# Heads exchanged in every second pair, and two output banks, in a retention layer ahead of two feed-forward layers

## The chip, the cores and the metric

One Trainium2 chip, one of its cores. The metric is device time in microseconds (us). A row of the profile comes from one profiled execution; the times of the table are those of separate timed runs.

## The reference, cut to what matters

Three layers follow each other on 2 x 768 = 1536 tokens of width 512 (8 heads of 64). Only the first one is touched by the change:

```python
def _attn_ref(q, k, v):            # each (2, 8, 768, 64)
    gamma = 1.0 - 2.0 ** (-5.0 - np.arange(H))
    for t in range(S):
        state = gamma * state + np.einsum('bhd,bhe->bhde', k[:, :, t], v[:, :, t])
        y[:, :, t] = scale * np.einsum('bhd,bhde->bhe', q[:, :, t], state)
# then x = y as (1536, 512);  h = x @ w_in (512 x 2048);  x = (h * tanh(softplus(h))) @ w_out
# then out = (sigmoid(x @ w_gate) * (x @ w_val)) @ w_out2    (512 x 1536 each way)
```

## The kernel before, in words

**The retention layer** is worked in chunks of 128 tokens, 12 of them (six to a batch element), numbered j = 0 to 11. Two heads make a pair, and a pair's two heads (e = 0 and 1) lie on partitions 0 to 63 and 64 to 127 of the tile `qk_t`; four pairs p = 0 to 3 lie side by side. For a chunk the kernel does this, all in plain fp32, and the trace counts two matmul instructions for each such product:

- `at_scores(j)`: the products of k and q, written to two PSUM banks `sc[e]`, 8 products (tile `sc`); on GpSimd, v times its decay (`vp`) and, from the second chunk of a batch element on, the output's decay (`og`); on VectorE the causal mask, which takes both banks to the tile `a`.
- `at_state(j)`: k times v is added to a running state in one bank (tile `st`), 8 products; ScalarE copies the state to SBUF as `s` for chunk j + 1. It is left out for the last chunk of a batch element (j = 5 and 11).
- `at_out(j)`: 8 products of `a` and `vp` go to one output bank `ao`, and, for all but the first chunk of a batch element (10 of the 12), 8 products of the state `s` and q are added to it, each of which uses 64 rows and 64 columns of the 128 x 128 array. VectorE then multiplies the bank with `og` into the activation tile `acc`, 128 x 512 in one instruction.

The output banks come from the pool `ps_o`, which has two buffers, one bank each. The same pool later holds the results of the feed-forward layers' second products (`o1_first`, `o1`, `o2`).

`blocks` runs four chunks at a time. For a chunk j it issues, in this order, `at_scores(j + 1)`, from j = 3 on one step of weight preparation (`pump`), `at_state(j)`, `at_out(j)`, the loads of chunk j + 4 and of a weight piece, and, from j = 4 on, one group of 12 matmuls of the first feed-forward layer (`dense`: tiles `h<-xc` and `h<-B`). The retention tiles of q, k and v have four buffers, so the loads for chunk j + 4 can start when chunk j has been used.

**A step of weight preparation** takes 512 x 128 weights that arrive as 64-bit floats (`raw`), decodes them (one instruction on ScalarE, three on VectorE, of which two are `SCALAR_TENSOR_TENSOR`), and splits the result into two fp32r halves (one copy `w` on ScalarE, one subtraction on VectorE).

**Order.** Through the whole retention stage each engine executes its instructions in program order (the class `InOrder`; in the profile these have the helper's line L66). Behind it (`early.clear`) a planner orders each engine's instructions at build time, and these rows have lines of their own (L109 is the matmul helper of the feed-forward layers). The first work behind the retention stage that uses `ps_o` is `out1_first(0)`, whose four steps `o1_first` take one bank each.

Of the kernel before, what the change touches and what calls it, by code (L numbers as in the profile page):

```python
# [9 lines left out]
F32 = mybir.dt.float32  # L10
# [4 lines left out]
ALU = mybir.AluOpType  # L15
PSUM = bass.MemoryType.PSUM

P = 128
# [4 lines left out]
def kernel(ctx, tc, qk, nv, w1i, w1o, w2g, w2v, w2o, ma_in, og_in, sg_in, ck_in, out):  # L23
# [14 lines left out]
    NP = KK  # L38
    D = P // 2
# [4 lines left out]
    SPC = N // P  # L44
# [27 lines left out]
    pe, dve, act, pool, sync = [InOrder(e) for e in (nc.tensor, nc.vector, nc.scalar, nc.gpsimd, nc.sync)]  # L72
# [8 lines left out]
    ps_o = ctx.enter_context(tc.tile_pool(name="ps_o", bufs=2, space=PSUM))  # L81
# [5 lines left out]
    acc_t = [big.tile([P, KK, N], F32, name=f"acc{c}") for c in range(NCH)]  # L87
# [354 lines left out]
    with ExitStack() as actx:  # L442
# [8 lines left out]
        qk_t, nv_t, a_t, vp_t, og_t, st_t, s_t = {}, {}, {}, {}, {}, {}, {}  # L451
# [32 lines left out]

        def at_out(j):
            a, v, t, s = a_t.pop(j), vp_t[j], qk_t[j], s_t.get(j)
            o = ps_o.tile([P, NP, P], F32, tag="o", name="ao")
            inter = j % SPB > 0

            for p in range(NP):  # L490
                for e in range(2):
                    pe.matmul(
                        out=o[D * e:D * e + D, p, :], lhsT=v[:, 2 * p + e, :], rhs=a[:, e, p, :],
                        start=p == 0, stop=p == NP - 1 and not inter, skip_group_check=True,
                    )
            if inter:
                for p in range(NP):
                    for e in range(2):
                        r = slice(D * e, D * e + D)
                        pe.matmul(  # L500
                            out=o[r, p, :], lhsT=s[r, p, :], rhs=t[r, 0, p, :], start=False, stop=p == NP - 1,
                            skip_group_check=True,
                        )
            dve.tensor_tensor(
                out=acc_t[j // SPC][:, :, j % SPC * P:j % SPC * P + P], in0=o, in1=og_t[j], op=ALU.mult
            )

        def at_state(j):
            if j % SPB == SPB - 1:
                return  # L510
            v, k = vp_t[j], nv_t[j]
            if j % SPB == 0:
                st_t[0] = ps_s.tile([P, NP, D], F32, tag="s", name="st")
            st = st_t[0]
            for p in range(NP):
                for e in range(2):
                    pe.matmul(
                        out=st[D * e:D * e + D, p, :], lhsT=k[:, 0, 2 * p + e, :], rhs=v[:, 2 * p + e, :],
                        start=j % SPB == 0 and p == 0, stop=p == NP - 1, skip_group_check=True,
                    )  # L520
            s_t[j + 1] = at.tile([P, NP, D], F32, tag="s", name="s")
            act.activation(out=s_t[j + 1], in_=st, func=AF.Copy)

        def fin(j):
            at_state(j)
            at_out(j)
# [22 lines left out]
        for n in range(WARM):  # L549
            o = ps_o.tile([P, NP * D], F32, tag="o", name="warm")  # L550
# [109 lines left out]
```

## Time and profile before

| | |
|---|---|
| timed runs | median 601.92 us, 600.83 to 603.3 (3 runs) |
| the profiled execution | 603.4 us, its span 601.6 us, so 1.8 us lie around the span |
| mean granted TensorE clock in the span | 0.993 |
| busy share of the span | TensorE matmuls 97%, VectorE 69%, GpSimd 55%, ScalarE 41% |

In the rows, PE is the matmuls of TensorE, PEld its weight loads, DVE is VectorE, ACT ScalarE, POOL GpSimd, SPq the queue that issues DMAs. A matmul row's duration is that of one instruction in a pipeline: rows overlap each other, so the pace is read from starts and not from durations. A tile's name stands as `out<-in`; a bracket behind a row gives the idle time of its engine just before it and what ended it. `issue` in a bracket means that the profile shows no wait that ended there.

### The profile page before, as it was taken

The numbers are of one execution on the slowest core, as the hardware profiler recorded it, in microseconds if no ns is written. First come the engines' busy times: TensorE is split into PE (matmuls) and PEld (weight loads), VectorE is DVE, ScalarE is ACT, GpSimd is POOL, SyncE is SP. The second block draws the span as 40 slices with busy tenths as digits, with TensorE's granted clock in tenths as the row PEclk, the third lists the DMA queues.
The fourth block names the chain that finished last, engine by engine and source line by source line (L and its number), as shares of the span: only waits on it lengthen the run. The fifth ranks groups of instructions, "written<-read, shape, count | busy, mean of one in ns | idle before, by whom it ended". The sixth has DMA issues, their size and how long they took to land.

```text
span 601.6 us, 7973 instructions
## 1 busy us (share of the span) xinstructions
PE 585.4 (97%) x3056; PEld 478.6 (80%) x3056; DVE 416.0 (69%) x572; ACT 249.5 (41%) x433; POOL 331.5 (55%) x268
## 2 busy tenths in 40 slices
PE   8998999999999999998999999999999999999997
PEld 7776787788787888886788787888888888888885
DVE  3899896438959485665776977686578487472554
ACT  1354456545454354443434645642333443333210
POOL 3345556628785585484632556955566657557100
PEclk9999899999999999998999999999999999999999
DMA  9983232204222122401220031133023033000014
GB/s 346 407 286 123 89 106 69 72 0 141 70 71 94 47 70 71 139 4 67 71 70 1 1 106 42 64 105 106 0 81 104 28 95 94 21 1 1 1 53 159
DMA packets 15591, 52.27 MB, mean 87 GB/s; under 512 B 1984, under 2 KB 2112, under 8 KB 15552
## 3 DMA queue, kind: packets, MB, share of 16 engines
q1 hardware_dynamic: 15552, 51.75, 25.0%
q8 instruction: 24, 0.39, 0.3%
q14 instruction: 15, 0.12, 0.1%
HBM read 48.60 MB, written 3.15 MB: 86 GB/s over the span
## 4 chain that ended last, share of the span: by engine, by line
PE 64%; DVE 15%; issue 7%; POOL 6%; DMA 4%; ACT 3%; SPq 0%; POOLq 0%; ACTq 0%; DVEq 0%
PE o L109 29%; PE h L109 27%; PE hx L109 7%; DVE v L102 3%; DMA nv_t<-nv 3%; DVE v L103 2%; DVE v L101 2%; DVE acc L357 2%; POOL w L163 1%; POOL vp L66 1%; POOL g L91 1%; DVE v L66 1%; POOL og L66 1%; POOL g L66 1%; DVE T L91 1%
## 5 line engine op out<-in xcount | busy, mean ns | idle before, releaser
L91 POOL TENSOR_TENSOR g<-e,g 128x512 fp32r<-128x512 f32 x73 | 116.5, 1605 | 86.7 <-ACT g L90 86.7
L109 PE MATMUL o<-g,w 128*128 128x512 f32 x576 | 141.8, 394 | 2.8 <-DVE acc L357 2.6
L109 PEld LDWEIGHTS o<-g,w 128*128 128x128 f32 x576 | 108.7, 190 | 28.2 <-DVE acc L357 5.1
L109 PE MATMUL h<-T,w 128*128 128x512 f32 x444 | 112.6, 390 | 1.1 <-DVE T L91 0.6
L163 POOL TENSOR_TENSOR w<-v,w 128x512 fp32r<-128x512 f32 x56 | 76.2, 1368 | 67.8 <-ACT w L162 67.6
L109 PE MATMUL o<-w,g 128*128 128x512 f32 x432 | 106.0, 390 | 0.0
L109 PEld LDWEIGHTS h<-T,w 128*128 128x128 f32 x444 | 83.2, 188 | 19.4 <-DVE T L91 1.0
L109 PEld LDWEIGHTS o<-w,g 128*128 128x128 f32 x432 | 81.0, 188 | 17.2 <-POOL g L91 0.4
L109 PE MATMUL h<-B,w 128*128 128x512 f32 x348 | 90.8, 390 | 0.8 <-DVE e L347 0.8
L109 PEld LDWEIGHTS h<-B,w 128*128 128x128 f32 x348 | 65.1, 188 | 15.1 <-DVE e L347 1.2
L357 DVE TENSOR_TENSOR acc<-o,acc 128x512 f32<-128x512 f32 x72 | 49.0, 686 | 39.1 <-PE o L109 38.8
L90 ACT ACTIVATE g<-e 128x512 fp32r<-128x512 f32 x77 | 48.1, 631 | 53.5 <-DVE e L347 35.5
L163 POOL TENSOR_TENSOR w<-s,w 128x512 fp32r<-128x512 f32 x34 | 48.1, 1422 | 34.5 <-ACT w L162 34.2
L101 DVE TENSOR_SCALAR v<-v 128x512 int32<-128x512 int32 x59 | 44.7, 761 | 28.2 <-ACT v L100 27.9
L162 ACT ACTIVATE w<-v 128x512 fp32r<-128x512 f32 x59 | 36.8, 631 | 63.0 <-DVE v L103 35.2
L377 DVE TENSOR_TENSOR acc<-o,acc 128x512 f32<-128x512 f32 x60 | 41.1, 686 | 30.8 <-PE o L109 30.4
L100 ACT ACTIVATE v<-raw 128x512 f32<-128x512 f32 x59 | 39.2, 669 | 52.5 <-POOL w L163 20.0
L102 DVE SCALAR_TENSOR_TENSOR v<-raw,v 128x512 int32<-128x512 int32 x59 | 56.0, 950 | 1.0
L103 DVE SCALAR_TENSOR_TENSOR v<-raw,v 128x512 int32<-128x512 int32 x59 | 56.2, 953 | 0.5
L109 PE MATMUL hx<-xc,w 128*128 128x512 f32 x216 | 55.7, 390 | 0.3 <-ACT e L341 0.3
L109 PE MATMUL h<-xc,w 128*128 128x512 f32 x216 | 55.0, 389 | 0.0
L109 PEld LDWEIGHTS hx<-xc,w 128*128 128x128 f32 x216 | 40.5, 188 | 9.2 <-ACT e L341 0.8
(78 smaller groups left out, 611.0 us busy)
## 6 DMA issues: line engine op xcount, KB each, us to landing
raw<-w1i SPq DMA_DIRECT2D x16, 512.0 KB, 3.6
raw<-w1o SPq DMA_DIRECT2D x16, 512.0 KB, 3.4
qk_t<-qk SPq DMA_DIRECT2D x12, 512.0 KB, 6.3
nv_t<-nv SPq DMA_DIRECT2D x12, 512.0 KB, 7.0
raw<-w2g SPq DMA_DIRECT2D x12, 512.0 KB, 3.3
raw<-w2v SPq DMA_DIRECT2D x12, 512.0 KB, 3.4
raw<-w2o SPq DMA_DIRECT2D x12, 512.0 KB, 3.3
out<-acc SPq DMA_DIRECT2D x12, 256.0 KB, 2.0
```

The lines of the kernel that those rows point to most:

```text
L66: i = call(**kw)
L90: act.activation(out=hi, in_=raw, func=AF.Copy)
L91: eng.tensor_tensor(out=lo, in0=raw, in1=hi.bitcast(F32), op=ALU.subtract)
L100: act.activation(out=v, in_=high.bitcast(F32), func=AF.Copy, scale=2.0 ** -112)
L101: dve.tensor_scalar(out=b, in0=b, scalar1=3, scalar2=None, op0=ALU.logical_shift_left)
L102: dve.scalar_tensor_tensor(out=b, in0=low, scalar=29, in1=b, op0=ALU.logical_shift_right, op1=ALU.bitwise_or)
L103: dve.scalar_tensor_tensor(out=b, in0=high, scalar=SIGN, in1=b, op0=ALU.bitwise_and, op1=ALU.bitwise_or)
L109: pe.matmul(out=o, lhsT=w(a), rhs=x(b), start=first and n == 0, stop=last and n == 2, skip_group_check=more)
L162: act.activation(out=hi, in_=v, func=AF.Copy)
L163: late.append(lambda: lo_eng["w"].tensor_tensor(out=lo, in0=v, in1=hi.bitcast(F32), op=ALU.subtract))
L357: dve.tensor_tensor(out=acc, in0=o, in1=acc, op=ALU.add)
L377: dve.tensor_tensor(out=acc, in0=o, in1=acc, op=ALU.add)
```

## The change

In pairs 1 and 3 the two heads change places among the partitions of `qk_t` (done on the host, when the input is laid out). So in those pairs the score bank `sc[e]` holds the other head, the running state is written to the other half of the array's columns, and a product of state and q reads rows of one half and writes columns of the other. In pairs 0 and 2 rows and columns are of the same half, as before. The eight products of state and q of a chunk thus use all four 64 x 64 quarters of the array. The output goes to two banks, pairs 0 and 2 to one, pairs 1 and 3 to the other, 256 columns each, so that no bank is written into the same partitions from both halves of the rows. Both come from `ps_o`. The multiplication with `og` becomes two instructions of 128 x 256, one for a bank.

```diff
         def at_out(j):
             a, v, t, s = a_t.pop(j), vp_t[j], qk_t[j], s_t.get(j)
-            o = ps_o.tile([P, NP, P], F32, tag="o", name="ao")
+            o = [ps_o.tile([P, NP // 2, P], F32, tag="o", name="ao") for _ in range(2)]
             inter = j % SPB > 0
             for p in range(NP):
                 for e in range(2):
                     pe.matmul(
-                        out=o[D * e:D * e + D, p, :], lhsT=v[:, 2 * p + e, :], rhs=a[:, e, p, :],
-                        start=p == 0, stop=p == NP - 1 and not inter, skip_group_check=True,
+                        out=o[p % 2][D * e:D * e + D, p // 2, :], lhsT=v[:, 2 * p + e, :], rhs=a[:, e ^ p % 2, p, :],
+                        start=p < 2, stop=p >= NP - 2 and not inter, skip_group_check=True,
                     )
             if inter:
                 for p in range(NP):
                     for e in range(2):
-                        r = slice(D * e, D * e + D)
+                        r = slice(D * (e ^ p % 2), D * (e ^ p % 2) + D)
                         pe.matmul(
-                            out=o[r, p, :], lhsT=s[r, p, :], rhs=t[r, 0, p, :], start=False, stop=p == NP - 1,
-                            skip_group_check=True,
+                            out=o[p % 2][D * e:D * e + D, p // 2, :], lhsT=s[r, p, :], rhs=t[r, 0, p, :],
+                            start=False, stop=p >= NP - 2, skip_group_check=True,
                         )
-            dve.tensor_tensor(
-                out=acc_t[j // SPC][:, :, j % SPC * P:j % SPC * P + P], in0=o, in1=og_t[j], op=ALU.mult
-            )
+            for n in range(2):
+                dve.tensor_tensor(
+                    out=acc_t[j // SPC][:, n::2, j % SPC * P:j % SPC * P + P], in0=o[n], in1=og_t[j][:, n::2],
+                    op=ALU.mult,
+                )
         def at_state(j):
...
             for p in range(NP):
                 for e in range(2):
+                    r = e ^ p % 2
                     pe.matmul(
-                        out=st[D * e:D * e + D, p, :], lhsT=k[:, 0, 2 * p + e, :], rhs=v[:, 2 * p + e, :],
+                        out=st[D * r:D * r + D, p, :], lhsT=k[:, 0, 2 * p + e, :], rhs=v[:, 2 * p + e, :],
                         start=j % SPB == 0 and p == 0, stop=p == NP - 1, skip_group_check=True,
                     )
...
     def feature_major(a):
-        a = a.reshape(B, H // 2, 2, nsub, P, D).transpose(0, 3, 2, 5, 1, 4)
+        a = a.reshape(B, H // 2, 2, nsub, P, D)
+        a = np.stack([a[:, p, ::1 - p % 2 * 2] for p in range(H // 2)], axis=1).transpose(0, 3, 2, 5, 1, 4)
         return a.reshape(B * nsub, 2 * D, H // 2, P)
```

## Rows read from the trace of the kernel before

**Rows 1.** The page's first part: busy us, share of the span, instructions.

```profile
PE 585.4 (97%) x3056; PEld 478.6 (80%) x3056; DVE 416.0 (69%) x572; ACT 249.5 (41%) x433; POOL 331.5 (55%) x268
```

**Rows 2.** Busy us (instructions) by stretch: PE, PEld, DVE, ACT, POOL; clock; DMA.

```profile
10.50:25.70 15.20, 14.54 (x260) 12.58 (x256) 10.44 (x16) 4.98 (x10) 8.99 (x9) 1.00 1.02 407
25.70:59.10 33.40, 29.26 (x302) 23.09 (x301) 31.58 (x42) 13.21 (x27) 14.52 (x11) 1.00 0.65 231
59.10:77.58 18.48, 18.47 (x181) 14.86 (x181) 15.46 (x20) 8.15 (x15) 9.10 (x7) 0.91 0.25 86
77.58:601.60 524.02, 514.39 (x2245) 421.01 (x2243) 355.65 (x491) 221.26 (x380) 296.38 (x235) 0.99 0.19 64
```

**Rows 3.** Timeline, chunk j = 2 on PE: start, us, what, count.

```profile
14.17 1.16 PE L66 MATMUL sc<-qk_t 64*128 64x128 f32 x16
...
15.26 0.69 PE L66 MATMUL st<-vp,nv_t 128*64 128x64 f32 x16
...
15.77 1.05 PE L66 MATMUL ao<-a,vp 128*64 128x128 f32 x16
...
16.75 1.09 PE L66 MATMUL ao<-qk_t,s 64*64 64x128 f32 x16
...
17.77 1.16 PE L66 MATMUL sc<-qk_t 64*128 64x128 f32 x16
```

**Rows 4.** Timeline of PE cut to 16.76 to 16.90 us.

```profile
16.75 0.33 PE L66 MATMUL ao<-qk_t,s 64*64 64x128 f32 x2
```

**Rows 5.** Timeline of ACT, 18 to 24 us.

```profile
19.52 0.70 ACT L66 ACTIVATE v<-raw 128x512 f32<-128x512 f32 x1 [3.08 <-DMA raw<-w1i]
...
22.73 0.36 ACT L66 ACTIVATE s<-st 128x256 f32<-128x256 f32 x1
```

**Rows 6.** Timeline of PE, 20 to 30 us: the state product of j = 4.

```profile
23.19 0.69 PE L66 MATMUL st<-vp,nv_t 128*64 128x64 f32 x16 [0.66 <-issue]
```

**Rows 7.** Timeline of DVE, 37.4 to 49.1 us: one chunk's work.

```profile
43.76 1.28 DVE L66 TENSOR_TENSOR a<-sc,ma 128x512 f32<-128x512 f32 x2
45.15 1.02 DVE L66 TENSOR_SCALAR v<-v 128x512 int32<-128x512 int32 x1
46.20 2.86 DVE L66 SCALAR_TENSOR_TENSOR v<-raw,v 128x512 int32<-128x512 int32 x2
48.98 0.68 DVE L66 TENSOR_TENSOR acc<-ao,og 128x512 f32<-128x512 f32 x1
```

**Rows 8.** Timeline of ACT, 56 to 60 us.

```profile
58.11 0.63 ACT L66 ACTIVATE w<-v 128x512 fp32r<-128x512 f32 x1 [4.33 <-DVE v L66]
58.65 0.37 ACT L66 ACTIVATE s<-st 128x256 f32<-128x256 f32 x1
```

**Rows 9.** Timeline of PE, 59 to 78 us: j = 9, 11, and out1_first.

```profile
59.11 0.69 PE L66 MATMUL st<-vp,nv_t 128*64 128x64 f32 x16 [2.40 <-issue]
...
60.76 1.97 PE L66 MATMUL ao<-qk_t,s 64*64 64x128 f32 x16
...
72.68 1.09 PE L66 MATMUL ao<-a,vp 128*64 128x128 f32 x16
...
77.58 0.62 PE L109 MATMUL o<-g,w 128*128 128x512 f32 x2
```

**Rows 10.** Timeline of DVE, 58 to 79 us: j = 10, 11 and behind.

```profile
67.32 1.29 DVE L66 TENSOR_TENSOR a<-sc,ma 128x512 f32<-128x512 f32 x2 [1.25 <-PE sc L66]
...
72.01 0.68 DVE L66 TENSOR_TENSOR acc<-ao,og 128x512 f32<-128x512 f32 x1
...
77.75 0.69 DVE L66 TENSOR_TENSOR acc<-ao,og 128x512 f32<-128x512 f32 x1
78.35 1.28 DVE L102 SCALAR_TENSOR_TENSOR v<-raw,v 128x512 int32<-128x512 int32 x2
```

**Rows 11.** PE alone by stretch: length, busy (instructions), granted clock, DMA.

```profile
60.38:63.79 3.41, 3.41 (x25) 0.50 0.14 55
```

**Rows 12.** Groups of DVE by form: the one of 256 columns.

```profile
L66 DVE MEMSET z<- 128x256 f32 x1 | 0.3, 272 | 0.0
```

## The prediction

> **What bounds the kernel now.** I read the page's totals first: PE is busy for 97% of the span, DVE for 69% [rows 1]. That mean hides the place of the change, so I cut the span at the borders of the retention stage [rows 2]. The change touches only what lies before 77.58 us, and there three stretches have three limits. From 10.5 to 25.7 PE is busy for 14.54 of 15.20 us, but the loads run at 407 GB/s with a DMA share of 1.02, so both are full. From 25.7 to 59.1 PE is idle for 4.1 us while DVE is busy for 31.58 of 33.40. From 59.1 to 77.58 PE is busy throughout (18.47 of 18.48), at a mean clock of 0.91. Behind that, PE idles for 9.6 us in 524 and sets the time: what PE gains or loses at 77.58 arrives at the end, unless one of those later waits takes it up.
>
> Then I followed each engine's timeline. On PE a chunk of the first stretch is four blocks of products without a gap, 3.60 us from scores to scores [rows 3]. ScalarE's first decode waited 3.08 us for its weights and started at 19.52 [rows 5]; the wait is a DMA's, not PE's. From there on VectorE's work for a chunk is a closed chain: mask 1.28, decode 1.02 and 2.86, eviction 0.68, with gaps of about 0.1 us or none between them [rows 7]. PE hangs on that chain: the state products of a chunk wait until ScalarE has copied the last state, and that copy stands behind the weight copy, which waited 4.33 us for VectorE's decode [rows 8]. So `st` of j = 4 came 0.66 us late [rows 6] and `st` of j = 9 came 2.40 us late [rows 9]. Only once in that part does VectorE wait for PE: 1.25 us for the last scores, because PE had started j = 9 late and then ran 3.41 us at a granted clock of 0.50, which is 1.2 GHz [rows 10, 11].
>
> **The change part by part: PE.** Eight products of state and q are 16 rows in 1.02 us, from 16.75 to the next scores at 17.77 [rows 3]. Now they go two at a time: two rows had started by 16.90 and no third [rows 4]. With four quarters, four can go together. Of the 1.02 us some 0.15 are the start and the change to the next block (the last row ends at 17.84 and lasts about as long as one of the 0.33 us in rows 4, so the starts are spread over some 0.8 us); the rest, 0.87, would halve: 0.44 saved per chunk, 4.4 us over the ten chunks that have these products. The lower bound is nothing, if the queue does not see far enough to fill four quarters; the upper is this half. I take 0.44. At the low clock it would be about twice that, since the block took 1.97 against 1.09 there [rows 3, 9].
>
> The Trainium skill (TensorEngine Tiling (Array Packing), section Key Properties) says that different tiles load weights and multiply in parallel, and counts four tiles of 64x64; by it the block takes half, which is the value taken above from the rows.
>
> The state products now write the array's column halves in the order 0, 1, 1, 0 in place of 0, 1, 0, 1. No row shows such an order. At best it costs nothing; at worst neighbours no longer overlap and the 0.51 us of that block [rows 3] doubles. I take nothing: the two column halves still get the same number of products. The products of `a` and `vp` keep their order and alternate halves; the second bank costs them nothing.
>
> **DVE.** One eviction of 512 columns becomes two of 256. One of 512 takes 0.68, two in a row 1.28 [rows 7], so a further one adds 0.60. A row of 256 columns that writes only takes 0.272 [rows 12]; twice that is 0.544, so 0.06 to 0.14 us of a 512-column instruction are fixed, and are now paid a second time. I take 0.10 per chunk, 1.2 us in all. Up to the `st` of j = 9 six evictions (j = 3 to 8) lie in VectorE's chain, of which the last runs beside that wait; about half of the other five meet a gap of 0.1 us like that before the decode [rows 7]. I take +0.3 us at 59.11.
>
> **The banks.** Before, a chunk used one of the pool's two banks, and the next chunk's products could start while the last bank was still being evicted. After, each chunk takes both, so the products of `a` and `vp` of chunk j + 1 wait for the eviction of chunk j. Behind them on PE stand the state-times-q products, the dense group and the next scores; VectorE's mask waits for those. Up to j = 10 an eviction is over before these products come. At j = 11 there is no cover: the eviction ran from 72.01 to 72.69 and PE came at 72.68 [rows 9, 10]. And `out1_first` needs a bank of the same pool at 77.58, while the last eviction runs from 77.75 to 78.44 [rows 9, 10]. Before, the other bank was free. After, PE waits there.
>
> **The sum.** Through j = 8 PE's savings go into its waits. In the first stretch the loads leave little to gain anyway, and the decode chain starts at 19.52 whatever PE does. The loads of chunk j + 4 are issued earlier, but into a full queue. So `st` of j = 9 comes at 59.11 + 0.3. The state-times-q of j = 9 gives back 0.44: the last scores and the mask behind them come 0.1 earlier, and so does the eviction of j = 10, which is 0.1 longer and ends where it did, at 72.7. The products of j = 11 therefore start at 72.75, 0.07 later than before, though PE is there 0.5 earlier. The last block gives 0.44: PE arrives at `out1_first` at 77.2. The last eviction starts at about 77.7 and its first half takes about 0.4; PE goes on at 78.15, which is 0.57 later than before. Nothing behind that is touched, so the end moves by +0.5 us, from 603.4 to 603.9 for the profiled execution. The median lies 1.5 us below that execution; from it I forecast 602.4.
>
> The rule that speaks against the change is the Trainium skill's in TensorEngine Tiling (Array Packing), section Performance Considerations, PSUM Bottleneck: tiling makes the products faster but not the emptying of the banks, which may become the limit. Rows 10 agree: what PE then waits for is the eviction. By the rule alone the time would not fall.
>
> **The rivals.**
>
> *The saving passes through.* If PE and not VectorE paces the chunks, ten times 0.44 less the 0.57 of the last wait is -3.8 us: 598.1. For it: PE is full from 10.5 to 25.7 and from 59.1. Against: DVE has no gap to give between 25.7 and 59.1, and PE already waits there.
>
> *Half of it:* the planner orders the rest so that PE does not wait at 77.2 (other products first), and VectorE's extra work is hidden. Then two or three savings remain, -0.9 to -1.3: 600.8.
>
> *The change does not do what it says:* the quarters are not filled. Then PE arrives 0.3 later at j = 9 and keeps that, the eviction of j = 10 is 0.4 late, the last one too, and PE goes on at 78.5: +0.9 us, 602.8. If the new order of the state products doubles their block as well, j = 9 adds 0.5: 603.3.
>
> *Slower:* the wait at `out1_first` grows and sets the clock down. Its place is the last eviction. There the planner may already put other decode work between VectorE's instructions; one more pair of 1.28 us like the one right behind it [rows 10] makes PE's wait 0.95 + 1.28 = 2.2 us. After a wait of 2.40 us the clock fell to 0.50 for 3.41 us [rows 9, 11], which costs 1.7 us of PE. Together 0.57 + 1.28 + 1.7 = +3.55: 605.5. It decides once such a pair goes ahead; without it the wait of 0.95 is near the 0.66 after which the clock stayed up [rows 2, 6].
>
> The Trainium skill (TensorE: Matmul & The Clock Gate, section HAM oscillation — how this bites in real kernels) says that idle gaps between bursts of matmuls bring the clock down. Rows 9 and 11 agree; it is the mechanism of this last rival.
>
> **How the numbers follow.** A measurement of this kernel can tell about 0.5% (3 us) from no change. Chances: the forecast 0.45 (+0.2 to +1.3, so 602.1 to 603.2), quarters not filled 0.11 and half of it 0.12, all three within 0.5%, so 0.68 for the same. The saving passing through has 0.15 (597.5 to 598.9). Slower has 0.17 (605 to 607), since the order of the 524 us behind the stage is set by a planner whose answer to new times I can't read from these rows; a wait of the same size anywhere in them costs the same. Faster by over 0.5%: 0.15. The range of 8 in 10 goes from 598.2 to 606.0, which leaves out about half of either outer case; the likeliest case alone spans 602.1 to 603.2.
>
> **What would show it.** The 16 rows of state times q should take about 0.6 us to the next block in place of 1.02, with four starts together. The eviction should be 24 rows of about 0.39 us. The wait before `st` of j = 9 should grow from 2.40 to about 3.5 us, since the blocks of j = 7 and 8 give 0.44 each and VectorE comes 0.3 later. PE should wait before the `a` and `vp` products of j = 11 and before the first `o`, released by the eviction. The forecast is wrong if VectorE's chain turns out to have been waiting for PE in the first 59 us, if the planner's order behind 77 us changes, or if stretches at the low clock come or go: each is worth 1.7 us.

## The result, and the profile after

The change makes the kernel slower. Its median is 606.61 us (606.12 to 607.63, 4 runs), that of the kernel before 602.12 us (600.83 to 603.3, 4 runs); the ratio is 1.007, 95% interval 1.0048 to 1.0093. The profiled execution took 606.3 us with a span of 604.5, against 603.4 and 601.6 before, so it shows 2.9 us of the 4.5. Up to the 1600th matmul (in order of their starts) it shows 4.42 us; then the profiled execution of before has a stretch at the low clock and that of after has not, though PE waits there alike, 2.28 us at 274.37 before and 2.29 us at 278.80 after. The same window of PE alone (length, busy time, granted clock, DMA share, GB/s), first before, then after; behind the wait in the kernel after the clock is 1.00, too:

```profile
275.42:278.83 3.41, 3.41 (x10) 0.50 0.12 47
275.42:278.83 3.41, 1.12 (x6) 1.00 0.39 120
```

Ratios compare the runs of two kernels as a whole and not their medians, so that the two need not agree in the last digit; both leave out two runs at a far lower mean clock, 972.94 us of the version e19 and 728.54 us of the kernel before on its chip.

The page's totals of the kernel after, as [rows 1]:

```profile
PE 581.4 (96%) x3056; PEld 474.0 (78%) x3056; DVE 419.8 (69%) x584; ACT 249.4 (41%) x433; POOL 327.8 (54%) x268
```

Its windows over the same stretches as [rows 2], with the same columns (the last is GB/s):

```profile
10.50:25.70 15.20, 13.29 (x258) 11.03 (x258) 10.54 (x20) 4.99 (x10) 8.78 (x9) 1.00 1.03 408
25.70:59.10 33.40, 27.56 (x302) 21.61 (x302) 31.90 (x47) 13.25 (x26) 14.53 (x11) 1.00 0.64 230
59.10:77.58 18.48, 17.26 (x180) 13.30 (x180) 16.05 (x23) 8.34 (x16) 9.09 (x7) 0.91 0.25 86
77.58:604.50 526.92, 514.61 (x2244) 421.03 (x2244) 358.09 (x491) 220.99 (x380) 292.74 (x235) 0.99 0.19 63
```

PE does the retention in less time: 1.25, 1.70 and 1.21 us less busy in the three stretches, with the same number of instructions to within two. VectorE is 0.3 to 0.6 us busier in the second and third. Yet the last stretch is 2.9 us longer, with the same work on PE.

**PE's blocks.** Timeline of PE, as [rows 3], for j = 1, with the j = 2 block cut at its start, as [rows 4], below it:

```profile
11.95 1.04 PE L66 MATMUL ao<-a,vp 128*64 128x128 f32 x16
12.92 0.67 PE L66 MATMUL ao<-qk_t,s 64*64 64x128 f32 x16
13.52 1.16 PE L66 MATMUL sc<-qk_t 64*128 64x128 f32 x16
...
16.10 0.45 PE L66 MATMUL ao<-qk_t,s 64*64 64x128 f32 x8
```

The block of state times q takes 0.60 us to the next scores where it took 1.02. The cut, 16.05 to 16.30 us, holds eight rows of it. The state products still take 0.52 (14.61 to 15.13), against 0.51 before [rows 3], so their new column order costs nothing.

**The waits of PE that the chain of VectorE sets**, as [rows 6, 9], and the block behind the second one at the low clock:

```profile
23.09 0.69 PE L66 MATMUL st<-vp,nv_t 128*64 128x64 f32 x16 [1.20 <-issue]
...
59.02 0.69 PE L66 MATMUL st<-vp,nv_t 128*64 128x64 f32 x16 [2.80 <-issue]
...
61.02 1.13 PE L66 MATMUL ao<-qk_t,s 64*64 64x128 f32 x16
```

The wait at j = 4 went from 0.66 to 1.20 us and that at j = 9 from 2.40 to 2.80: PE comes earlier, and leaves 0.10 and 0.09 us earlier. At 59 us seven chunks have had such a block (j = 1 to 5, 7 and 8), and nearly all that they saved, 7 x 0.42 = 2.9 us, has gone into waits.

**The handover**, where the retention stage ends and the first output products of the feed-forward layers (`o<-g,w`) begin. Timeline of PE in the kernel after, as [rows 9]:

```profile
71.64 2.20 PE L109 MATMUL h<-B,w 128*128 128x512 f32 x9
73.77 1.09 PE L66 MATMUL ao<-a,vp 128*64 128x128 f32 x16
74.80 0.67 PE L66 MATMUL ao<-qk_t,s 64*64 64x128 f32 x16
75.39 0.96 PE L109 MATMUL h<-B,w 128*128 128x512 f32 x3
78.87 7.37 PE L109 MATMUL o<-g,w 128*128 128x512 f32 x24 [2.52 <-DVE acc L66]
...
89.03 2.88 PE L109 MATMUL o<-g,w 128*128 128x512 f32 x12
92.86 0.50 PE L109 MATMUL o<-g,w 128*128 128x512 f32 x1 [0.95 <-ACT acc L365]
```

Timeline of VectorE in the kernel after, as [rows 10]:

```profile
71.47 0.74 DVE L66 TENSOR_TENSOR acc<-ao,og 128x256 f32<-128x256 f32 x2
...
77.20 1.29 DVE L102 SCALAR_TENSOR_TENSOR v<-raw,v 128x512 int32<-128x512 int32 x2
78.40 0.75 DVE L66 TENSOR_TENSOR acc<-ao,og 128x256 f32<-128x256 f32 x2
```

The planner has changed the order on two engines. Nine of the twelve dense matmuls that stood behind chunk 11 now stand ahead of it, so the wait for the bank of j = 10 is covered. And the pair of decode instructions that stood behind the last eviction (78.35 in [rows 10]) now stands ahead of it. PE is done with everything else at 76.35 and waits 2.52 us for the bank. Then the clock falls, as in [rows 11]; the window of PE alone in the kernel after:

```profile
80.40:83.82 3.42, 3.42 (x10) 0.50 0.80 262
```

The 24 output products take 7.37 us where those 24 took 5.60 before. PE then meets a second wait, 0.95 us at 92.86, for a copy-out on ScalarE (L365, the instruction that empties an output bank of the feed-forward layers). A wait of PE for a bank to be emptied is called a gate below. Timeline of ScalarE in the kernel after:

```profile
83.13 0.60 ACT L365 ACTIVATE acc<-o 128x512 f32<-128x512 f32 x1 [0.66 <-PE o L109]
...
91.67 0.66 ACT L100 ACTIVATE v<-raw 128x512 f32<-128x512 f32 x1 [7.42 <-POOL s L176]
92.23 0.58 ACT L365 ACTIVATE acc<-o 128x512 f32<-128x512 f32 x1
```

The same of the kernel before, where both copy-outs stand ahead of that decode copy:

```profile
82.00 0.58 ACT L365 ACTIVATE acc<-o 128x512 f32<-128x512 f32 x1
...
83.52 0.59 ACT L365 ACTIVATE acc<-o 128x512 f32<-128x512 f32 x1
...
93.95 0.66 ACT L100 ACTIVATE v<-raw 128x512 f32<-128x512 f32 x1 [7.63 <-POOL s L176]
```

After, the second copy-out is ordered behind the decode copy (L100, the first step of decoding a weight), which waits for GpSimd's sums; the second bank was full at about 86.2 us and is emptied at 92.23.

The balance: 2.52 of wait, 7.37 - 5.60 = 1.77 of low clock and 0.95 of the second wait are 5.24 us; PE reached the first output products 77.58 - 76.35 = 1.23 us earlier; so it should be 4.0 us late behind the second wait. Counted by matmuls, the 850th, between the two waits, starts 3.06 us later than before (2.52 + 1.77 - 1.23) and the 880th, behind the second, 4.31. Later waits of both kernels then move the difference: 3.08 us at the 1000th, 4.42 at the 1600th, 2.85 at the 1700th, behind the stretch near 275 us.

### The profile page after: what moved, and what is told of

The parts are those of the page before. It is cut to its first block, busy times and chain, and to the rows that moved or that the text cites. A ratio compares the mean times of both kernels' runs of the same rounds, so it can differ in the third digit from the quotient of the medians.

```text
span 604.5 us, 7985 instructions
## 1 busy us (share of the span) xinstructions
PE 581.4 (96%) x3056; PEld 474.0 (78%) x3056; DVE 419.8 (69%) x584; ACT 249.4 (41%) x433; POOL 327.8 (54%) x268
## 4 chain that ended last, share of the span: by engine, by line
PE 72%; DVE 11%; issue 7%; POOL 4%; ACT 2%; DMA 2%; SPq 0%; POOLq 0%; ACTq 0%
PE o L109 32%; PE h L109 30%; PE hx L109 8%; DVE v L102 2%; DVE v L103 2%; DVE v L101 1%; DMA nv_t<-nv 1%; DVE acc L357 1%; POOL w L163 1%; DVE v L66 1%; POOL vp L66 1%; POOL og L66 1%; PE ao L66 1%; DVE T L91 1%; DMA qk_t<-qk 1%
## 5 line engine op out<-in xcount | busy, mean ns | idle before, releaser
L91 POOL TENSOR_TENSOR g<-e,g 128x512 fp32r<-128x512 f32 x73 | 112.2, 1546 | 96.0 <-ACT g L90 95.9
L100 ACT ACTIVATE v<-raw 128x512 f32<-128x512 f32 x59 | 39.4, 670 | 56.0 <-POOL s L176 21.2
L103 DVE SCALAR_TENSOR_TENSOR v<-raw,v 128x512 int32<-128x512 int32 x59 | 60.1, 1018 | 0.6
L102 DVE SCALAR_TENSOR_TENSOR v<-raw,v 128x512 int32<-128x512 int32 x59 | 55.5, 942 | 1.1
L109 PEld LDWEIGHTS h<-xc,w 128*128 128x128 f32 x216 | 40.6, 188 | 8.4
```

The lines of the kernel that those rows point to most:

```text
L91: eng.tensor_tensor(out=lo, in0=raw, in1=hi.bitcast(F32), op=ALU.subtract)
L100: act.activation(out=v, in_=high.bitcast(F32), func=AF.Copy, scale=2.0 ** -112)
L102: dve.scalar_tensor_tensor(out=b, in0=low, scalar=29, in1=b, op0=ALU.logical_shift_right, op1=ALU.bitwise_or)
L103: dve.scalar_tensor_tensor(out=b, in0=high, scalar=SIGN, in1=b, op0=ALU.bitwise_and, op1=ALU.bitwise_or)
L109: pe.matmul(out=o, lhsT=w(a), rhs=x(b), start=first and n == 0, stop=last and n == 2, skip_group_check=more)
```

## The experiments

The theory after the result: both output banks held by the last chunk make PE wait for an eviction, and the planner's answer to that (evictions late, copy-out behind the decode copy) does the rest; the exchange of heads is innocent. Rivals: the exchange itself, the longer VectorE work, or the low clock alone. Every ratio below is to runs of the kernel before on the same chip as the version's own, with a 95% interval; medians of different versions come from different chips.

### e1: one bank less held at the end

```diff
-            o = [ps_o.tile([P, NP // 2, P], F32, tag="o", name="ao") for _ in range(2)]
+            o = [ps_o.tile(..., tag="o", name="ao") for _ in range(2 if j < NSUB - 1 else 1)]
+            if j == NSUB - 1:
+                o.append(ps_s.tile([P, NP // 2, P], F32, tag="s", name="ao"))
```

> The changed kernel, but chunk 11 takes its second output bank from the state's pool, which is free by then, so one bank of the output pool is free for the first feed-forward results. Theory A (the bank is held: PE waits 2.52 us at the first output products, and the clock falls behind that wait): the wait goes, the low stretch at 80.4 us goes, and the time falls by 2.5 + 1.7 us to about 602.5. Theory B (the planner's changed order from 71 us on is what costs, whoever holds the bank): the order of the last eviction and of the products of chunk 11 is still that of the changed kernel, so the time stays within 1 us of 606.6. Theory C (the exchanged heads cost in the array): stays at 606.6.

602.24 us, ratio 0.9989 [0.9977, 1.0002]. Timeline of PE in this version:

```profile
76.31 5.71 PE L109 MATMUL o<-g,w 128*128 128x512 f32 x24
```

Timeline of its VectorE:

```profile
77.34 1.28 DVE L102 SCALAR_TENSOR_TENSOR v<-raw,v 128x512 int32<-128x512 int32 x2
78.54 0.75 DVE L66 TENSOR_TENSOR acc<-ao,og 128x256 f32<-128x256 f32 x2
```

The order around chunk 11 is that of after, the last eviction is even later (78.54), and nothing waits for it: the output products start at 76.31, with no low clock behind them, and ScalarE's two copy-outs stand ahead of the decode copy (81.99 and 83.51). The loss is gone. So it is the held bank that makes a late eviction matter. That the time is not below that of before is a matter of later waits: PE is 1.15 us ahead of the kernel before at the 850th matmul and only 0.54 ahead at the 1600th, since it waits 0.40, 0.59 and 0.35 us for VectorE's evictions between 184 and 227 us; between 110 and 270 us the kernel before has none above 0.16.

### e6: the second bank of every chunk from another pool

```diff
+            o = [ps_o.tile([P, NP // 2, P], F32, tag="o", name="ao"),
+                 ps_h.tile([P, NP // 2, P], F32, tag="h", name="ao")]
```

> The changed kernel, but the second bank of every chunk comes from the five banks of the scores and first products; the output pool gives one bank per chunk as before. The heads stay exchanged, the eviction stays in two halves. Theories A and B: no wait at the first output products, the order is nearly that of the kernel before, time 601 to 602.5. If the saving of 0.42 us per chunk reaches the end through the last three chunks it is 601. Theory C: 606. A new wait for the five banks would show as PE waiting before scores.

602.33 us, ratio 0.9994 [0.9982, 1.0007]. The planner's order around chunk 11 is that of before, the output products start at 77.34 without a wait. The same answer by another way.

### e2: the banks without the exchange

The kernel before, with its output in two banks of `ps_o` and the eviction in two instructions, heads as they were:

```diff
-            o = ps_o.tile([P, NP, P], F32, tag="o", name="ao")
+            o = [ps_o.tile([P, NP // 2, P], F32, tag="o", name="ao") for _ in range(2)]
...
-                        out=o[r, p, :], lhsT=s[r, p, :], ...
+                        out=o[p % 2][r, p // 2, :], lhsT=s[r, p, :], ...
```

> The kernel before, with the two output banks and the eviction in two halves, and without the exchange of heads. Theories A and B: the loss is there without the exchange, 606 to 607.5 (the saving on PE, 0.4 us in the last chunks, is missing). Theory C: about 602.5, since only the eviction has grown, by 0.07 us per chunk.

608.72 us, ratio 1.0105 [1.0082, 1.0127], with the two waits of the kernel after. Timeline of PE in this version:

```profile
79.27 5.73 PE L109 MATMUL o<-g,w 128*128 128x512 f32 x24 [1.70 <-DVE acc L66]
...
93.22 4.46 PE L109 MATMUL o<-g,w 128*128 128x512 f32 x12 [2.55 <-ACT acc L365]
```

The banks alone make the loss. Here the clock stays up behind the first wait and falls behind the second (0.50 from 94.46 to 97.87). On top of the banks the exchange looks like a help of 0.35%, some 2 us, by the two ratios (and 2.06 us at the 1600th matmul of the profiles), but the intervals overlap.

### e3, e7, e15: the order held

The kernel after, with every later VectorE and TensorE instruction issued behind the last retention instruction of its engine:

```diff
             call = getattr(self.engine, name)
             if not early:
-                return call
+                if self not in (pe, dve):
+                    return call
+
+                def behind(**kw):
+                    with tc.issue_after(self.last):
+                        return call(**kw)
+
+                return behind
```

> The changed kernel, but everything on VectorE and TensorE behind the retention stage is ordered behind that stage's last instruction on the same engine, so that the planner can no longer put decode work before the last eviction or dense products before chunk 11. Both banks are still held. Theory A in the form of the prediction: PE waits about 0.5 to 1 us at the first output products, too short for the clock to fall; time about 602.5. Theory that holding both banks costs by itself whatever the order: a wait of 2 us or more and a low stretch stay, 605 or more.

602.16 us, ratio 1.0004 [0.999, 1.0018]. Timeline of PE in this version:

```profile
72.13 1.12 PE L73 MATMUL ao<-a,vp 128*64 128x128 f32 x16 [0.23 <-DVE acc L73]
...
77.24 5.74 PE L67 MATMUL o<-g,w 128*128 128x512 f32 x24 [0.45 <-DVE acc L73]
```

Both banks are still held, and the last eviction stands early. Timeline of its VectorE:

```profile
76.77 0.75 DVE L73 TENSOR_TENSOR acc<-ao,og 128x256 f32<-128x256 f32 x2
```

This costs PE 0.23 and 0.45 us. These are the two small waits that the prediction had expected (there about 0.5 and 0.95). So holding the banks costs little with an early eviction; the rest hangs on the order.

The same edit on the kernel before is its partner:

> The kernel before with the same fence behind the retention stage, as the partner of the fenced changed kernel (602.16 us): with the order held, the difference of the two is what the change costs without the planner. Forecast's own sum: the fenced changed kernel is 0.3 to 0.8 us slower than this one, so this one is 601.4 to 602.4. Theory that the order and not the bank is the loss: within 0.3 us of each other.

603.49 us, ratio 1.002 [1.0006, 1.0034]: the order held is no gain of its own. The forecast for the pair is missed: the changed kernel is not 0.3 to 0.8 us slower than its partner but 0.16% faster by the ratios, with intervals that overlap. And the held order with one bank less at the end:

> The changed kernel with the fence and with the last chunk's second bank from the state's pool, so neither the order nor the held bank is left. The waits of the fenced kernel before the first output products (0.45 us) and before chunk 11 (0.23 us; that one is chunk 10's bank and stays) go in part: 0.4 us below the fenced changed kernel, some 0.2 to 0.6 us below the fenced kernel before.

602.97 us, ratio 1.0009 [0.9995, 1.0023]; PE waits 0.94 us at 71.90 for the eviction of j = 10 and reaches the output products at 76.66 without a wait. PE gets there 0.6 us earlier than in the version of e3 and the end does not move by an amount that can be told, so the 0.4 us expected of it are not shown.

### e11: the first wait filled

The kernel after, with 20 matmuls whose result nobody reads, 256 columns each, ahead of the first output products:

```diff
+        fill = ps_s.tile([P, NP * D], F32, tag="s", name="fill")
+        for n in range(20):
+            pe.matmul(out=fill, lhsT=b_t["B11"][:, 0, 0, :P], rhs=b_t["B11"][:, 0, 0, :NP * D])
```

> The changed kernel with 20 products of 256 columns that nobody reads, put on TensorE ahead of the first output products, to fill the 2.5 us wait there. The wait for the bank stays, only idling goes. Theory A (the wait is dear because the clock falls behind it, 3.41 us at half speed): no low stretch at 80 us and 1.7 us less than the changed kernel, about 604.9. Theory that the wait alone and the following order make the loss: still 606.6. If the products run on past the end of the wait, up to 0.5 us is lost again.

608.69 us, ratio 1.0109 [1.0091, 1.0127]: a miss, slower than the kernel after. Timeline of PE in this version:

```profile
75.16 2.54 PE L564 MATMUL fill<-B 128*128 128x256 f32 x20
78.56 5.74 PE L109 MATMUL o<-g,w 128*128 128x512 f32 x24 [0.87 <-DVE acc L66]
...
92.51 4.38 PE L109 MATMUL o<-g,w 128*128 128x512 f32 x12 [2.77 <-ACT acc L365]
```

Timeline of its ScalarE:

```profile
91.31 0.66 ACT L100 ACTIVATE v<-raw 128x512 f32<-128x512 f32 x1 [8.15 <-POOL s L176]
91.88 0.58 ACT L365 ACTIVATE acc<-o 128x512 f32<-128x512 f32 x1
```

The clock stays up at the first output products, and what PE gained is lost at the second copy-out, where it comes at about the same time as in the kernel after (92.51 against 92.86), waits 2.77 us, and runs at 0.57 from 92 to 96 us. There are two gates in a row. Shortening the first alone gives nothing.

### e18, e19: the second gate taken away

The kernel after, with the decode copy issued behind the second copy-out, and the step of weight preparation between the two groups moved behind the second:

```diff
-        act.activation(out=v, in_=high.bitcast(F32), func=AF.Copy, scale=2.0 ** -112)
+        with tc.issue_after(second[0]) if second else nullcontext():
+            act.activation(out=v, in_=high.bitcast(F32), func=AF.Copy, scale=2.0 ** -112)
...
-        act.activation(out=acc_t[c][:, d, :], in_=o, func=AF.Copy)
+        i = act.activation(out=acc_t[c][:, d, :], in_=o, func=AF.Copy)
+        if (c, d) == (0, 2):
+            second.append(i.ins)
```

> The kernel after, with one order set on ScalarE: the copy-out of the second group of first output products (c=0, d=2) must stand ahead of the next decode copy, which waits for GpSimd's sums until 91.6 us. Theory (the second gate is that place in ScalarE's queue): both copies end before 88 us, the wait of 0.95 us for the copy-out at 92.86 us is gone, the wait of 2.52 at the first output products and the low clock behind it stay; about 0.95 us less than after, 605.7 us. Rival (the gate is the decode copy and GpSimd itself, wherever the copy-out stands: the dense products need the decoded weights next): no gain, 606.6 us or more, with a wait for a weight some 5 to 10 us later in its place.

602.38 us, ratio 1.0009 [0.9994, 1.0023]: more than either theory gave. Timeline of PE in this version:

```profile
78.15 5.72 PE L112 MATMUL o<-g,w 128*128 128x512 f32 x24 [1.58 <-DVE acc L66]
...
87.79 5.60 PE L112 MATMUL o<-g,w 128*128 128x512 f32 x24
```

Timeline of its ScalarE:

```profile
87.10 0.58 ACT L368 ACTIVATE acc<-o 128x512 f32<-128x512 f32 x1
87.57 1.23 ACT L103 ACTIVATE v<-raw 128x512 f32<-128x512 f32 x2
```

Timeline of its VectorE:

```profile
77.08 0.68 DVE L105 SCALAR_TENSOR_TENSOR v<-raw,v 128x512 int32<-128x512 int32 x1
77.68 0.75 DVE L66 TENSOR_TENSOR acc<-ao,og 128x256 f32<-128x256 f32 x2
```

The second wait is gone. But the edit moved the first one too: only one instruction of the decode pair still stands ahead of the last eviction, which comes at 77.68 in place of 78.40; PE waits 1.58 us, and the clock stays at 1.00. And it moved GpSimd's work: the four sums that the decode copy waits for lie there between 79.20 and 85.4, in the kernel after between 88.69 and 91.6, so the second gate went in two ways at once. So this run alone doesn't separate the parts. With the fill as well:

> The same order on ScalarE together with the 20 unread matmuls of 256 columns ahead of the first output products. Theory (two gates in a row, each hiding the other): the fill keeps the clock up, the second twelve output products start at about 89.6 us in place of 92.86, so about 3.2 us less than after, 603.4 us, where the fill alone gave 608.7. Rival (GpSimd's late sums and the decode behind them hold PE whatever stands ahead): 606 to 609 us, with the wait at a weight decoded behind GpSimd's sums.

601.98 us, ratio 1.0004 [0.9989, 1.0019]. Against the fill alone this is 1.05% less, and the fill adds nothing to the set order.

### e20, e21: the late eviction put back, without the second gate

The version of e18 with unread clears on VectorE ahead of the last eviction, two and three of them:

```diff
+            if j == NSUB - 1:
+                y = at.tile([P, NP * D], F32, tag="s", name="y")
+                for n in range(2):
+                    dve.memset(ap=y, constant=0.0)
             for n in range(2):
                 dve.tensor_tensor(
```

> The kernel of the set copy-out order, and ahead of the last eviction two unread clears of 256 columns on VectorE (0.27 us each before), so that the last eviction comes some 0.5 us later than its 77.68 and PE's wait for it at the first output products, 1.58 there, grows to about 2.1, without the wait for the second copy-out. Theory (the loss was the second gate; a late eviction is taken up by waits that PE has later anyway): 602.4 to 603.0 us. Rival (wait and low clock at the first output products count by themselves): 602.4 + 0.5 for the wait, and 1.7 more if the clock falls behind it, 604.6 us.

603.6 us, ratio 1.0024 [1.0012, 1.0035]. PE waits 2.02 us and starts the output products at 78.40 with the clock up. The two theories lay too near each other here; the interval overlaps that of e18.

> The same with three unread clears, before which the planner also puts two more decode instructions of 0.69 us: the last eviction some 2.0 us later than 77.68, PE's wait for it about 3.6 us in place of 1.58, longer than the 2.52 of the kernel after, and no wait for the second copy-out. Theory (the second gate was the loss): 602.4 to 603.5 us, although wait and low clock are there. Rival (wait and low clock count by themselves): 602.4 + 2.0 + 1.7 = 606.1 us.

605.97 us, ratio 1.005 [1.0032, 1.0068]: the rival was right. Timeline of PE in this version:

```profile
80.28 7.30 PE L112 MATMUL o<-g,w 128*128 128x512 f32 x24 [3.44 <-DVE acc L66]
...
90.37 5.60 PE L112 MATMUL o<-g,w 128*128 128x512 f32 x24
```

Its window of PE alone behind that wait (busy time, granted clock, DMA):

```profile
80.28:84.50 4.22, 4.22 (x12) 0.60 0.34 129
```

The last eviction comes at 79.87 in place of 77.68; the planner also put one more decode instruction and a weight's subtraction ahead of it. There is no second wait here. The first one is 3.44 - 1.58 = 1.86 us longer than in e18, the 24 products 7.30 - 5.72 = 1.58 longer, together 3.44; the spans of the two profiled executions differ by 4.0, the medians by 3.6, the ratios by 0.41%, 2.5 us. So wait and clock reach the end where no second gate takes them up: in full by the profiles, and by the ratios in the main.

### e8, e9, e5, e4: VectorE's chain

Whether the exchange is worth more where VectorE doesn't pace the chunks was tried in two ways. First, the third decode instruction of VectorE (the sign) is left out for the weights that are decoded in the retention stage, in the kernel before and in the version of e1; their weights lack the sign:

```diff
-        dve.scalar_tensor_tensor(out=b, in0=high, scalar=SIGN, in1=b, ...)
+        if not early:
+            dve.scalar_tensor_tensor(out=b, in0=high, scalar=SIGN, in1=b, ...)
```

> The kernel before, with the last of the three VectorE instructions of a decode left out in the retention stage (the weights prepared there lose their sign), so that VectorE's chain per chunk is 0.7 to 1.4 us shorter. Theory D (VectorE's chain paces the chunks from 20 to 59 us and swallows what PE saves): the stage gets shorter by most of the 9 x 1.0 us left out, about -6 us, 596. Theory E (PE paces the chunks): no change, 602.

> The same decode left out, on the changed kernel with the last chunk's second bank from the state's pool. Theory D: with VectorE's chain shorter PE waits less for it, and part of the 0.42 us per chunk now reaches the end: 1 to 3 us below the same without the exchange. Theory E': the saving does not come through for another reason (loads, ScalarE's queue): the two are within 0.7 us of each other.

595.86 us, 0.99 [0.9881, 0.9919], and 595.74 us, 0.9875 [0.9854, 0.9897]. One VectorE instruction per chunk less takes 6 to 7 us off the kernel before, and PE fills the middle of the stage (window with all engines, the kernel before without that instruction, against 29.26 of 33.40 in [rows 2]):

```profile
25.70:59.10 33.40, 32.03 (x352) 25.78 (x352) 29.16 (x42) 15.29 (x29) 17.71 (x14) 1.00 0.67 248
```

So the decode on VectorE did pace the stage. The exchange adds 0.25% by the ratios, but their intervals overlap, so neither theory of e9 is shown.

Second, the weights' subtraction goes from VectorE to GpSimd, without and with the exchange (and the bank of e1):

```diff
-    lo_eng = {"w": dve, "g": pool}
+    lo_eng = {"w": pool, "g": pool}
```

> The kernel before, with the weights' subtraction of the retention stage on GpSimd in place of VectorE (0.69 us per weight less on VectorE, 1.3 us more on GpSimd). Theory D: some 3 us faster, about 599, if GpSimd's extra work does not slow VectorE's decode. If VectorE's two decode instructions, which take 0.71 us when GpSimd is idle and 1.43 when it is busy, get slower in turn, no gain: 602.

> The same move of the subtraction on the changed kernel with the last chunk's second bank from the state's pool. Theory D: at least as fast as the same without the exchange, by 0 to 2 us. If the planner's order puts the last eviction behind decode work again, as in the changed kernel, without a wait for the bank it costs nothing.

603.16 us, 1.0003 [0.999, 1.0016], and 602.98 us, 1.0004 [0.9993, 1.0016]. Neither moves, a miss where 599 was expected of the former. VectorE now waits for ScalarE's decode copy in place of doing the subtraction. Timeline of VectorE in the version of e5:

```profile
46.35 1.03 DVE L66 TENSOR_SCALAR v<-v 128x512 int32<-128x512 int32 x1 [0.89 <-ACT v L66]
```

Timeline of ScalarE in the kernel before:

```profile
44.44 0.68 ACT L66 ACTIVATE v<-raw 128x512 f32<-128x512 f32 x1
```

There, too, that copy ends (45.12) just before VectorE's decode starts (45.15 [rows 7]). So by these rows two chains of nearly one length pace the middle of the stage: VectorE's own, and one that goes from VectorE's decode through ScalarE's queue to the next decode copy. The instruction left out in e8 lies in both, the subtraction only in the first, and from one pair of decode instructions to the next it is 6.62 us in e5 (40.80 to 47.42) and 6.61 before (39.59 to 46.20).

## Why the prediction was wrong

**Right: the four quarters.** 1.02 to 0.60 us per chunk is 0.42 where 0.44 was taken, and 0.84 at the low clock.

**Right: the column order costs nothing, and the evictions a little.** Two of 256 columns take 0.74 us where one of 512 took 0.68, so +0.06 where 0.10 was taken.

**Right in kind, small in size: the savings go into PE's waits.** The wait before j = 9 is 2.80, where about 3.5 was expected, and PE leaves it at 59.02, 0.09 earlier than before, not 0.3 later. Part of the saving went into other waits on the way: the scores wait 0.60 us for the load of `qk_t` at 20.72, and the state products at 43.39 wait 1.37 (0.93 at 43.49 before). The runs with the lighter chain confirm that the decode paced the stage. The +0.3 us for the evictions is missing at 59.02; that the second chain, which has no eviction in it, covers them is argued from e5, not shown.

**Wrong: the bank at j = 11.** PE was expected to wait there to 72.75. Nine dense matmuls were put ahead instead, and PE came to the first output products at 76.35, not at 77.2. Where the order was held, the forecast wait was there (0.23 us at 72.13).

**The step that failed** is "The last eviction starts at about 77.7 and its first half takes about 0.4; PE goes on at 78.15", with "Nothing behind that is touched". The eviction started at 78.40, behind a pair of decode instructions, PE went on at 78.87, and two things behind it were touched: the clock fell (1.77 us), and ScalarE's second copy-out went behind a decode copy that starts at 91.67 (0.95 us). The prediction took the order of before for that of after, though it knew that a planner makes that order anew. With the order held on PE and VectorE the forecast's time comes out, 602.16 us, but that confirms little: against its partner with the same order (e7) the +0.5 us of the sum is not there.

**The slower rival was the one that came**, with its place (the last eviction), its condition (one more pair of 1.28 us ahead of it) and its clock. It was priced at 0.57 + 1.28 + 1.7 = 3.55 and given 0.17. At the first gate alone the measured price is 3.06. What it lacked is the second gate, which the rows of before don't show, because there both copy-outs stand ahead of the decode copy. With the gate, the price is 5.24 less 1.23 that PE comes earlier. That the median then lies within the rival's 605 to 607 is in part luck, since the waits behind the gates and the stretch near 275 us move the difference between 2.9 and 4.4 us. The Trainium skill (TensorE: Matmul & The Clock Gate, section HAM oscillation — how this bites in real kernels) says that idle gaps between bursts of matmuls bring the clock down. These traces agree in part: 0.50 behind the waits of 2.40, 2.52, 2.55, 2.80 and 3.44 us, but 1.00 behind the 2.29 us at 278.80 in the kernel after, and 1.00 behind a wait in the version of e11 as long as one that brought it down in the kernel after (timeline of its PE; the granted clock is 1.00 from there to 67.20). In the version of e15 it fell behind a wait of 1.20 us at 23.27 (0.50 for 3.41 us from 23.54).

```profile
59.04 0.69 PE L66 MATMUL st<-vp,nv_t 128*64 128x64 f32 x16 [2.79 <-issue]
```

So such a wait doesn't settle by its length alone whether the clock falls, and the rival's clock term of 1.7 us was a chance and not a price.

The Trainium skill (TensorEngine Tiling (Array Packing), section Restrictions and Gotchas, PSUM Pressure) warns that row tiling takes more PSUM, since different row tiles write different banks. The runs agree: the banks alone make the loss, ratio 1.0105.

**What the loss is made of.** Shown: it needs both banks held (e1, e6 without, e2 with), and an order that makes the wait long (e3). Shown: the wait and the low clock count by themselves, 1.86 of wait and 1.58 of clock against 4.0 us in the profiled spans and 2.5 by the ratios (e21), and the second gate takes back what is won at the first (e11; e19, where the order on ScalarE and GpSimd's sums both changed, gives it again). Not shown: why the planner chose this order. That ScalarE's second copy-out is put behind the decode copy in answer to a later expected time for the output banks is argued from e1 and e6, which differ from the kernel after only in where one bank comes from and keep the copy-outs ahead. Also open is how much of the exchange would reach the end: 0.35% on top of the banks and 0.25% with a lighter chain, both with overlapping intervals, and nothing that can be told in e15 against e7.

No version that computes the same result was found to beat the kernel before by more than can be told: the nearest is that of e1, 0.9989 [0.9977, 1.0002].

## What to carry to other kernels

A second PSUM buffer for a tile is paid by whoever comes next in that pool: before taking both banks of a pool, find the last holder and the first follower, and price the wait with the eviction as late as the scheduler may put it, not where it stands now. Where an order is planned anew at each build, a small change of one due time can turn into two gates, as here; hold the order around the change (or compare the order of each engine before any time) and only then judge the change. A saving on an engine that waits for another's chain was worth nothing here while that chain kept its length; leaving out one instruction shows cheaply what paces, but look whether a second chain of the same length stands beside it.

## What the runs showed that was not expected

GpSimd and VectorE seem to hold each other up strongly behind the stage; no run isolates it. One GpSimd subtraction of 512 columns, 1.28 us at 73.93 in the version of e18, took 9.56 us from 79.17 in the kernel after (9.36 from 81.66 before) beside an unbroken row of VectorE work; the sums, and the decode copy behind them, come after it. Timeline of GpSimd in the kernel after:

```profile
79.17 9.56 POOL L91 TENSOR_TENSOR g<-e,g 128x512 fp32r<-128x512 f32 x1 [4.17 <-ACT g L90]
```

In the version of e18 GpSimd's sums stood first, at 79.20, and it was VectorE's subtractions that grew: a pair took 2.38 and the next 2.93 us where pairs take 1.29 in the kernel after.

The decode pair on VectorE takes 2.86 us in the stage [rows 7] and 1.28 behind it, by form the same instructions. In the kernel before GpSimd is at work beside the first (45.84 to 48.52), and idle beside the pairs that start at 20.74 (1.42) and 78.35 (1.28).
